# Splitting the first loads of a long-convolution block with a gated FFN, and writing its instruction order anew

## The chip, the cores and the metric

The kernel runs on one core of one Trainium2 chip. Its time is the device time of one execution in microseconds; where several executions were timed, the median is given.

## The reference

The input is a sequence of 2048 rows of 640 values (`q`, also the residual), with `k` and `v` of the same shape. With `LN` a layer norm without weights:

```python
q  = LN(x)                                   # x is A_q
ks = sum over t < 4 of shift(k, t) * shift_k[:, t]   # short causal convolution
kv = ks * v
y  = causal convolution of kv with ssm_k along the sequence + kv * ssm_D   # by FFT in the reference
h  = x + q * y
h2 = h + (silu(LN(h) @ w_gate) * (LN(h) @ w_up)) @ w_down   # 640 -> 1728 -> 640
```

Each of the 640 channels has its own filter `ssm_k` of 2048 taps. All tensors are bfloat16.

## The kernel before

The sequence is cut into four blocks of 512 rows, each laid over 128 partitions with four rows (r = 0 to 3) in each. The long convolution is done by blocks: each block of `kv` (X0 to X3) and of the filter (g0 to g3, transposed on TensorE by L431, the last by DMA) is taken to a spectrum of 512 real rows by matmuls with a table `WF` (L352), spectra are multiplied on VectorE (L591, L612, L615), summed over the pairs that meet in an output block, and taken back by matmuls with a table `WI` (L745). The short convolution is a set of small matmuls: `k`, transposed into a tile `T` (L533 and the copies L537 for block 0, DMA transposes for the others), times diagonal matrices `diag` that hold the taps (L978); the result times `v` is `kv`, made either by VectorE straight from PSUM (L578) or by a ScalarE copy (L579) and a VectorE product (L580). What TensorE leaves in PSUM goes to SBUF by ScalarE (L344, L435) or VectorE (L345, L435).

For block 0 the two spectra (X0, G0) and their products are worked in two halves of 320 channels, so that the first half can be multiplied while the second is transformed. The layer-norm sums are ScalarE's (L671, L628), their small arithmetic VectorE's (L643 to L653), the application either engine's (L682, L685).

Each finished block j goes through the FFN (f0 to f3): `LN(h)` is transposed (L783 on TensorE, L776 by DMA), multiplied by the gate and up weights (L846), passed through SiLU and product (L835, L837, L840), and multiplied by `w_down` (L915, L900). The FFN of block j - 1 is woven into the spectral work of block j; f3 comes last and alone.

Every instruction group is first entered into a list (`plan.add`, with an engine, an estimated length, and what it reads and writes). The table `ORDER` then gives the order in which the groups are issued; a negative number picks a group's other engine (VectorE in place of ScalarE, an accumulating DMA of GpSimd in place of a VectorE sum). Each engine runs its own instructions in that order. The large tiles share 13 slots (`big`), four PSUM tiles (`ps`) serve all matmuls, and a slot is handed out in the order of the table. So a new table changes the order on every engine, some engines, and the slots. The loads stand in the same table: `load` issues from SyncE's queue, and with an alternative from GpSimd's. SyncE issues in order, and an issue that waits for its slot holds up those behind it.

At the start TensorE turns over 34 idle matmuls (L959) until `k` has landed. Then come the transposes of `k`, those of g0, the short convolution, and the first forward transforms. In this kernel `k`, `g`, `v` and `WF` are loaded by one DMA each; `load_t` can cut a load by rows r, and `GPIECES` cuts the first g by groups of 128 channels, of which there are five.

Of the kernel before, what the change touches and what calls it, by code (L numbers as in the profile page):

```python
# [19 lines left out]
P = 128  # L20
# [18 lines left out]
GPIECES = ((0, KT),)  # L39
# [150 lines left out]
def kernel(ctx: ExitStack, tc: tile.TileContext, A_q, A_k, A_v, A_shift_k, A_ssm_k, A_ssm_D, B_x,  # L190
# [34 lines left out]
    def pe(ns, fn, r, w, holds=(), late=338):  # L225
        op = plan.add("pe", ns, fn, r, w, holds)
        op.late = late
        return op
# [278 lines left out]
    def load_k(j):  # L507

        if j == 0:
            return load_t(kk, 0)  # L510
# [471 lines left out]
    first("Lx0")  # L982
    x = load_x(0)
    first("Lv0")
    v = load_t(vv, 0)
    first("LWF")
    load(P * R * 4 * P * 2, 4096, lambda: nc.sync.dma_start(out=ap(WF), in_=wf_h.ap()), [WF])
    first("Lg0")
# [115 lines left out]
```

## Time and profile before

| | us |
|---|---|
| median of 3 runs | 257.15 (256.29 to 257.36) |
| profiled execution | 256.16 |
| its span, first to last instruction | 254.4 |
| mean granted TensorE clock | 0.993 |

The profile is one execution. A page gives the busy time of each engine: PE is TensorE's matmuls, PEld its weight loads (they overlap), DVE VectorE, ACT ScalarE, POOL GpSimd; SP is SyncE, which only issues DMAs. A row of the timeline gives the start, the length, the engine, the line of the kernel, the operation with its tiles (out<-in), and how often it was repeated; in square brackets the idle time ahead of it and what ended it. Rows of equal instructions that follow each other are merged.

### The profile page before, as it was taken

How to read it: one execution, taken by the hardware profiler on the slowest of the kernel's cores; microseconds unless marked ns; L12 is line 12 of the kernel's file. 1: busy time of each engine (PE TensorE's matmuls, PEld its weight loads, DVE VectorE, ACT ScalarE, POOL GpSimd, SP SyncE). 2: the span in 40 equal slices, each digit the busy share in tenths (PEclk: the TensorE clock that was granted, in tenths of full speed). 3: DMA queues.
4: the chain of work that ended last, by engine and by line, in shares of the span. 5: the costliest groups of instructions: out<-in, count | busy, mean ns of one | idle time of the engine just before them, and what ended most of it. 6: DMA issues, size and time to landing. Idle time of an engine off the chain costs nothing.

```text
span 254.4 us, 5139 instructions
## 1 busy us (share of the span) xinstructions
PE 246.7 (97%) x2070; PEld 145.2 (57%) x2070; DVE 192.1 (76%) x280; ACT 174.9 (69%) x306; POOL 67.4 (27%) x73
## 2 busy tenths in 40 slices
PE   8699999999999999999999999999999999999994
PEld 7566667744555576645554567544447744444663
DVE  0599999999989999999979999999998300102213
ACT  3969999998679899686788984348668144635200
POOL 6300020113444011149932013136920024000000
PEclk9799999999999999999999999999999999999999
DMA  6999777998897979898976386989973229000011
GB/s 239 350 356 234 196 203 141 211 249 199 159 330 199 176 169 183 205 200 207 278 142 119 83 126 119 187 192 212 211 158 80 58 46 131 0 0 0 3 41 62
DMA packets 51906, 41.04 MB, mean 161 GB/s; under 512 B 25461, under 2 KB 46202, under 8 KB 51882
## 3 DMA queue, kind: packets, MB, share of 16 engines
q1 hardware_dynamic: 45040, 26.94, 41.5%
q0 software_dynamic: 6832, 13.77, 30.5%
q8 instruction: 16, 0.26, 0.4%
q14 instruction: 8, 0.07, 0.1%
q10 hardware_dynamic: 10, 0.01, 0.0%
HBM read 22.03 MB, written 4.59 MB: 105 GB/s over the span
## 4 chain that ended last, share of the span: by engine, by line
PE 86%; ACT 6%; DMA 3%; DVE 2%; issue 1%; SPq 0%; DVEq 0%
PE ps L846 46%; PE ps L915 22%; PE ps L352 7%; ACT S L344 5%; PE ps L745 4%; PE ps L570 4%; DMA big<-in_A_ssm_k_dram 3%; PE ps L431 1%; PE ps L900 1%; DVE big L578 1%; ACT big L435 1%; ACT row L628 1%; DVE S L345 1%; ACT row L685 0%; ACT big L785 0%
## 5 line engine op out<-in xcount | busy, mean ns | idle before, releaser
L846 PE MATMUL ps<-big,big 128*128 128x512 bf16 x540 | 120.6, 379 | 0.0
L846 PEld LDWEIGHTS <-big 128*128 128x128 bf16 x540 | 52.0, 98 | 60.1 <-issue 0.5
L915 PE MATMUL ps<-wd,tT 128*128 128x320 bf16 (+2 forms) x416 | 59.5, 299 | 0.0
L915 PEld LDWEIGHTS <-tT 128*128 128x128 bf16 x416 | 40.3, 98 | 16.8 <-issue 1.3
L352 PE MATMUL ps<-big,WF 128*128 128x320 bf16 x224 | 37.0, 298 | 1.1 <-ACT S L344 0.4
L344 ACT ACTIVATE S<-ps 128x640 bf16<-128x640 f32 (+1 forms) x62 | 33.4, 620 | 4.3 <-PE ps L352 4.0
L612 DVE TENSOR_TENSOR big<-S,S 128x2560 bf16<-128x2560 bf16 x24 | 34.8, 1486 | 0.7 <-DMA S<-big 0.4
L835 ACT CAST co<-ps 128x1024 bf16<-128x1024 f32 x24 | 24.1, 1016 | 15.3 <-PE ps L846 15.1
L837 ACT ACTIVATE tT<-ps 128x1024 bf16<-128x1024 f32 x24 | 24.6, 1024 | 13.8 <-PE ps L846 13.7
L352 PEld LDWEIGHTS <-WF 128*128 128x128 bf16 x224 | 21.4, 97 | 12.7 <-issue 3.2
L628 ACT ACTIVATE row<-big 128x640 bf16<-128x640 bf16 x32 | 23.8, 752 | 2.2 <-DVE big L762 1.2
L840 DVE TENSOR_TENSOR tT<-tT,co 128x2048 bf16<-128x2048 bf16 x12 | 14.7, 1222 | 13.0 <-ACT co L835 9.0
L615 DVE TENSOR_TENSOR S<-S,big 128x2560 bf16<-128x2560 bf16 x16 | 23.4, 1486 | 0.1
L256 POOL DMA_DIRECT2D S<-big x9 | 10.9, 1210 | 46.0 <-DVE big L612 14.6
L685 ACT ACTIVATE row<-big,sm 128x640 bf16<-128x640 bf16 x22 | 19.6, 928 | 2.7 <-DVE sm L653 1.7
L858 DVE TENSOR_TENSOR tT<-tT,co 128x512 bf16<-128x512 bf16 x4 | 1.7, 422 | 21.7 <-ACT tT L856 21.3
L925 POOL DMA_DIRECT2D out_dram<-row x12 | 12.1, 1314 | 17.3 <-ACT row L924 17.2
L256 POOL DMA_DIRECT2D S<-S x4 | 5.7, 1431 | 38.2 <-ACT S L344 38.2
L924 ACT CAST row<-ps 128x640 bf16<-128x640 f32 x12 | 8.1, 690 | 10.3 <-PE ps L900 6.6
L759 DVE SCALAR_TENSOR_TENSOR row<-row,ps 128x640 bf16<-128x640 bf16 x16 | 12.8, 818 | 3.1 <-PE ps L745 2.9
L570 PEld LDWEIGHTS <-T 64*128 64x128 bf16 x640 | 12.0, 113 | 4.2 <-issue 4.0
L570 PE MATMUL ps<-diag,T 64*128 64x64 bf16 x640 | 13.5, 198 | 0.0
(93 smaller groups left out, 276.1 us busy)
## 6 DMA issues: line engine op xcount, KB each, us to landing
S<-big POOLq DMA_DIRECT2D x9, 640.0 KB, 6.3
big<-in_B_w_gate_dram SPq DMA_DIRECT2D x11, 320.0 KB, 5.6
big<-in_B_w_up_dram SPq DMA_DIRECT2D x10, 320.0 KB, 6.6
big<-in_A_q_dram SPq DMA_DIRECT2D x4, 640.0 KB, 5.5
big<-in_A_ssm_k_dram SPq DMA_DIRECT2D x4, 640.0 KB, 7.0
big<-in_A_v_dram SPq DMA_DIRECT2D x4, 640.0 KB, 4.3
S<-S POOLq DMA_DIRECT2D x4, 640.0 KB, 6.8
wd<-in_B_w_down_dram SPq DMA_DIRECT2D x1, 2080.0 KB, 12.2
```

The costliest lines, as they stand in the source:

```text
L256: nc.gpsimd.dma_start(out=to(), in_=what(), accum_op=ALU.add, max_dma_last_dim=2 * D * 2)
L344: plan.add("act", 700 if n else 430, lambda: nc.scalar.activation(dst(), src(), ACT.Copy, scale=by), [ps], [part], (), ("dve", 820 if n el ...
L352: nc.tensor.matmul(ap(ps)[:, h, 0:NH], ap(WF)[:, c, r, :], ap(src)[:, r, h * NH:(h + 1) * NH], start=(first and i == 0), stop=(last and i ...
L570: nc.tensor.matmul(out()[:, b, c, :], k, ap(diag)[at, c, t, :], start=(t == 0), stop=(t == 3))
L612: dve(1490, lambda b=b, xs=xs, hs=hs: nc.vector.tensor_mul(flat2(b), X.part(xs), H.part(hs)), [X.at(xs), H.at(hs)], [b], [A.b])
L615: f(A.part(dst), A.part(dst), flat2(b))
L628: act(825, lambda r=r, junk=junk: nc.scalar.activation(ap(junk), ap(x)[:, r, :], ACT.Square, scale=D ** -0.5, accum_out=sm(s, 1)[:, r:r + ...
L685: nc.scalar.activation(ap(row), ap(x)[:, r, :], ACT.Identity, bias=sm(s, 5)[:, r:r + 1], scale=sm(s, 4)[:, r:r + 1])
L835: act(1010, lambda ps=ps: nc.scalar.copy(ap(co)[:, at:at + 2, :], ap(ps)), src, [(co, gi % 2)])
L837: act(1010, lambda ps=ps: nc.scalar.activation(ap(tT)[:, c:c + 2, :], ap(ps), ACT.Silu), src, [done(range(c, c + 2), ROWS)])
L846: nc.tensor.matmul(ap(ps)[:, i, :], ap(w)[:, k, off:off + P], ap(hT)[:, k, :], start=(k == 0), stop=(k == KT - 1))
L915: nc.tensor.matmul(ap(ps)[:, hf, 0:n], ap(tT)[:, c, at:at + P], ap(wd)[:, c, col:col + n], start=j % 2 == 0 and c == order[0], stop=j % 2 ...
```

## The change

Four things change in the code. The first `k` and the first `v` are loaded in two pieces each (rows r = 0, 1 and rows 2, 3). The first `g` is loaded in two pieces, channel groups 0 and 1, and 2 to 4; its transposes wait for their own piece. `WF` is loaded in two pieces, table rows c = 0, 1 and c = 2, 3; a forward matmul waits for its half. The table `ORDER` is new throughout: it was searched for again with a model of the engines in which early pauses of TensorE count against an order. That search's model is not part of the kernel.

```diff
-GPIECES = ((0, KT),)
+GPIECES = ((0, 2), (2, KT))
...
 ORDER = [
-    0, 4, 2, 15, 1, 16, 5, 6, 19, 22, 20, 24, 26, 17, 18, 3, 23, 344, 9, 7, -26, -11, 28, -15, 353, 44, 29, 12, 200, 13,
...
+    16, 1, 15, 4, 23, 22, 0, 2, 5, 9, 6, 28, 7, 17, 32, 24, 30, 21, 3, 33, 19, 26, -30, -15, 55, 11, 20, 49, 31, 27, 48, 34,
...
-        pe(136 * len(ws) * len(rs), mm, [(src, r) for r in rs] + [WF] + ([] if first else [ps]), [ps], holds)
+        pe(136 * len(ws) * len(rs), mm, [(src, r) for r in rs] + [(WF, c // 2)] + ([] if first else [ps]), [ps], holds)
...
-            return load_t(kk, 0)
+            return load_t(kk, 0, 2)
...
-    v = load_t(vv, 0)
+    v = load_t(vv, 0, 2)
     first("LWF")
-    load(P * R * 4 * P * 2, 4096, lambda: nc.sync.dma_start(out=ap(WF), in_=wf_h.ap()), [WF])
+    for c in (0, 2):
+        load(P * R * 2 * P * 2, 2048, lambda c=c: nc.sync.dma_start(out=ap(WF)[:, c:c + 2], in_=wf_h.ap()[:, c:c + 2]), [(WF, c // 2)])
```

The lines of the new kernel stand one or two lower than those of the old (L352 becomes L353, L846 becomes L847, L987 becomes L989).

The table of numbers tells a reader little; the order on the engines tells more. First SyncE's queue at the start of the program, before. `big_72` takes k, `big_73` x (A_q), `big_74` g, `big_75` v.

```order
L317 DMA big_72<-in_A_k_dram 128x2560
L323 DMA big_73<-in_A_q_dram 128x2560
L309 DMA big_74<-in_A_ssm_k_dram 128x5x512
L317 DMA big_75<-in_A_v_dram 128x2560
L987 DMA WF<-const_wf 128x2048
L807 DMA big_76<-in_B_w_up_dram 128x5x256
L807 DMA big_77<-in_B_w_up_dram 128x5x256
L309 DMA big_79<-in_A_ssm_k_dram 128x5x512
```

The same place of SyncE's queue now; `big_73` takes g and `big_74` x.

```order
L318 DMA big_72<-in_A_k_dram 128x1280 x2
L310 DMA big_73<-in_A_ssm_k_dram 128x3x512
L310 DMA big_73<-in_A_ssm_k_dram 128x2x512
L324 DMA big_74<-in_A_q_dram 128x2560
L989 DMA WF<-const_wf 128x1024
L318 DMA big_75<-in_A_v_dram 128x1280
L989 DMA WF<-const_wf 128x1024
L318 DMA big_75<-in_A_v_dram 128x1280
L310 DMA big_78<-in_A_ssm_k_dram 128x5x512
```

g stands ahead of x, the halves of WF and v alternate, and the two early weight loads (`w_up`) have gone further back.

Second, VectorE from its first copy of `T` to the first normalisation steps, before. `big_78` is the transposed g, `big_80` kv, `S_64` and `S_65` the spectra of g and kv.

```order
L537 COPY T<-ps_93 128x5x128
L978 TENSOR_SCALAR diag<-row_88,taps 128x64 x8
L537 COPY T<-ps_95 128x5x128
L549 MEMSET T 128x20
L435 COPY big_78<-ps_94 128x640
L435 COPY big_78<-ps_96 128x640
L435 COPY big_78<-ps_94 128x640
L437 TENSOR_TENSOR big_78<-big_78,row_87 1x640
L435 COPY big_78<-ps_95 128x640
L578 TENSOR_TENSOR big_80<-ps_96,big_75 128x2x5x64
L578 TENSOR_TENSOR big_80<-ps_94,big_75 128x2x5x64
L345 TENSOR_SCALAR S_64<-ps_93 128x320
```

VectorE at the same place now; `big_76` is the transposed g, `big_77` kv.

```order
L538 COPY T<-ps_96 128x5x128
L979 TENSOR_SCALAR diag<-row_87,taps 128x64 x12
L436 COPY big_76<-ps_96 128x640
L550 MEMSET T 128x20
L436 COPY big_76<-ps_93 128x640
L436 COPY big_76<-ps_94 128x640
L438 TENSOR_TENSOR big_76<-big_76,row_88 1x640
L436 COPY big_76<-ps_95 128x640
L346 TENSOR_SCALAR S_64<-ps_94 128x320
L579 TENSOR_TENSOR big_77<-ps_96,big_75 128x2x5x64
L346 TENSOR_SCALAR S_64<-ps_94 128x320
L579 TENSOR_TENSOR big_77<-ps_93,big_75 128x2x5x64
```

One copy of T has gone to ScalarE, four products for `diag` have come from GpSimd, and a first eviction of g's spectrum stands ahead of the first product with v. Up to the end of block 0's inverse VectorE has eight evictions of this kind where it had six, and four products straight from PSUM where it had three.

Third, SyncE's queue where block 2's loads begin, now. `big_76` is a slot of FFN weights of block 0 that takes the next v, `big_73` and `big_84` are slots of later FFN weights, `big_79` takes x of block 2.

```order
L518 DMA_TRANSPOSE T<-in_A_k_dram 128x5x128 x3
L324 DMA big_79<-in_A_q_dram 128x2560
L318 DMA big_76<-in_A_v_dram 128x2560
L808 DMA big_84<-in_B_w_gate_dram 128x5x64
L808 DMA big_73<-in_B_w_gate_dram 128x5x256
L1028 DMA wd<-in_B_w_down_dram 64x640
```

Before, at that place:

```order
L517 DMA_TRANSPOSE T<-in_A_k_dram 128x5x128
L820 DMA out_dram<-big_73 128x2560
L807 DMA big_83<-in_B_w_up_dram 128x5x256
L309 DMA big_76<-in_A_ssm_k_dram 128x5x512
L807 DMA big_77<-in_B_w_gate_dram 128x5x256
L1023 DMA wd<-in_B_w_down_dram 128x13x640
```

The load of v for block 2 now stands ahead of two weight loads for the FFN of block 0. Between the last matmul on the old contents of `big_76` and the first on `big_73` TensorE has 30 FFN matmuls (L847) and 80 convolution matmuls. Late in the program, ahead of the first inverse matmul of block 3 (L745, now L746), TensorE has 130 of the 135 gate and up matmuls of f2, where it had 125, and VectorE one more product L840 (now L841) and one more sum L762 (now L763).

79 rows, old and new, of the table ORDER are left out of this document.

## The prediction

> **What bounds the kernel now.** I read the page's busy shares first, then the busy time of each engine in stretches cut where the shares change. The columns of a stretch are its length, then busy us (and instructions) of each engine, the granted TensorE clock, and the DMA share.
>
> ```profile
> PE 246.7 (97%) x2070; PEld 145.2 (57%) x2070; DVE 192.1 (76%) x280; ACT 174.9 (69%) x306; POOL 67.4 (27%) x73
> ...
> 5.00:9.40 4.40, 2.37 (x35) 1.94 (x35) 2.20 (x12) 3.11 (x8) 3.90 (x10) 0.96 0.97 333
> 9.40:12.60 3.20, 3.20 (x77) 2.92 (x75) 1.28 (x3) 3.20 (x10) 0.00 (x0) 0.52 1.08 362
> 12.60:30.00 17.40, 16.37 (x216) 11.11 (x209) 16.97 (x36) 15.26 (x40) 0.00 (x0) 1.00 1.11 288
> 30.00:50.00 20.00, 19.54 (x296) 14.37 (x294) 19.49 (x42) 19.63 (x36) 2.49 (x2) 1.00 0.83 169
> 50.00:190.00 140.00, 140.00 (x1063) 76.37 (x1061) 135.69 (x154) 107.97 (x178) 52.59 (x46) 1.00 0.88 188
> ```
>
> TensorE is busy 97% of the span, and from 50 us on without a gap, so nothing can be gained there; a new order can only lose. What can be gained lies in three places ahead of 50 us. Up to 9.4 TensorE stands idle for 2.0 of 4.4 us. From 9.4 to 12.6 it is busy but at 0.52 of its clock. From 12.6 to 50 VectorE (16.97 of 17.40, 19.49 of 20.00) and ScalarE are as full as TensorE: there the PSUM evictions and the spectral products pace it, and its "busy" holds waits inside the pipeline. The timeline of the front shows why.
>
> ```profile
> 0.79 0.40 SPq L317 DMA_DIRECT2D big<-in_A_k_dram  x1
> 1.25 0.41 SPq L323 DMA_DIRECT2D big<-in_A_q_dram  x1
> 1.72 0.43 SPq L309 DMA_DIRECT2D big<-in_A_ssm_k_dram  x1
> 2.18 0.75 SPq L317 DMA_DIRECT2D big<-in_A_v_dram  x1
> 2.98 0.45 SPq L987 DMA_DIRECT2D WF<-const_wf  x1
> 3.78 5.12 POOL L978 TENSOR_SCALAR diag<-row,taps 128x64 bf16<-128x64 bf16 x12 [1.26 <-DVE taps L970]
> 4.99 1.33 PE L533 MATMUL ps<-ident,big 128*128 128x128 bf16 x15
> 5.76 0.70 ACT L537 COPY T<-ps 128x640 bf16<-128x640 bf16 x1 [2.88 <-PE ps L533]
> 6.07 0.49 DVE L537 COPY T<-ps 128x640 bf16<-128x640 bf16 x1 [2.48 <-PE ps L533]
> 6.48 1.25 DVE L978 TENSOR_SCALAR diag<-row,taps 128x64 bf16<-128x64 bf16 x8
> 8.78 0.52 PE L431 MATMUL ps<-ident,big 128*128 128x128 bf16 x5 [1.83 <-DMA big<-in_A_ssm_k_dram]
> 9.23 1.25 PE L570 MATMUL ps<-diag,T 64*128 64x64 bf16 x40
> 10.41 1.79 PE L431 MATMUL ps<-ident,big 128*128 128x128 bf16 x15
> 12.65 0.47 DVE L437 TENSOR_TENSOR big<-big,row 1x640 bf16<-1x640 bf16 x1
> 13.45 1.53 DVE L578 TENSOR_TENSOR big<-ps,big 128x640 bf16<-128x640 f32 x2
> 13.57 1.16 PE L352 MATMUL ps<-big,WF 128*128 128x320 bf16 x6
> 16.48 0.76 PE L570 MATMUL ps<-diag,T 64*128 64x64 bf16 x40
> ```
>
> TensorE transposes k from 4.99, waits 1.83 us for g, and then meets the slow clock: 40 convolution matmuls take 1.25 us at 9.23 and 0.76 at 16.48. The first forward-transform matmul (L352) starts at 13.57, and VectorE's long unbroken run starts with the product at 13.45. When the loads land, the issues tell (last number: us from issue to landing).
>
> ```profile
> big<-in_A_k_dram SPq DMA_DIRECT2D x1, 640.0 KB, 3.9
> big<-in_A_q_dram SPq DMA_DIRECT2D x1, 640.0 KB, 5.1
> big<-in_A_ssm_k_dram SPq DMA_DIRECT2D x1, 640.0 KB, 7.0
> big<-in_A_v_dram SPq DMA_DIRECT2D x1, 640.0 KB, 8.1
> ...
> WF<-const_wf SPq DMA_DIRECT2D x1, 512.0 KB, 8.7
> ```
>
> Issue plus landing time: k at 4.7, q at 6.35, g at 8.7, v at 10.3, WF at 11.7. They come one after another: q 1.65 us after k, g 2.4 after q (its packets are shorter), v 1.6, WF 1.4.
>
> **The change part by part.** *The loads.* The new SyncE order is k in two pieces, g in two, q, then halves of WF and v in turn. With g straight behind k, its first piece (3 of 5 parts) lands about 4.7 + 1.45 = 6.1 and its second at 4.7 + 2.4 = 7.1, 1.6 us earlier; q then at 8.75, WF's first half at 9.45, v's first at 10.25, WF's second at 10.95, v's second at 11.75. The extra issues cost about 0.4 us each on SyncE's queue and all stand ahead of the data: with two more ahead of them g's last piece is issued at about 2.2. What a split costs in landing the trace does not show. From below it is nothing or a little gain (the 640 KB loads follow each other without a gap); from above I take one SyncE issue per piece, 0.45 us, and 0.9 for k and g together. I take nothing: g has that much cover, as the next step shows.
>
> *The front.* VectorE now does 12 of the diag products (1.25/8 = 0.156 each) and one copy of T; GpSimd does 8 instead of 12, and is done by 3.78 + 8 x 0.427 = 7.2. ScalarE does three T copies: 6.07 + 3 x 0.70 = 8.17. VectorE: T copy from 5.76 to 6.25, diag to 8.13, first g copy (0.49) to 8.62, a memset to 8.7, two more g copies to 9.68, the row addition 0.47 to 10.15, the last copy to 10.64. The g transposes are paced by PSUM buffers that these copies free, the last behind ScalarE's copy at 8.17, so g could land at 8.0 and cost nothing. The first convolution starts at 8.7, the second at 9.46, the first forward matmul at 10.2 against 13.57. VectorE's long run starts at 10.65 against 13.45: a lead of **2.8 us**. It needs v's first half at 11.1 (lands 10.25) and WF's second half near 11.8 (lands 10.95): covered, each by 0.8. GpSimd now issues a 320 KB weight load at about 7.3, right behind its diag products, which shares the DMA engines with these halves: half of q's 1.65 us, 0.8, if all of it went ahead, just the cover; the two w_up loads that stood behind WF on SyncE before come later instead.
>
> *The clock.* Before, the 1.83 us ahead of 8.78 are empty. Now the 20 g transposes fall there (5 took 0.52) and the convolution at 8.7 follows, so I expect no slow stretch. If it comes all the same, two convolutions take 1.25 instead of 0.76; VectorE's queue hides most of it, so the cost lies between 0 and 0.5 us. I take 0.
> The rule of the Trainium skill (TensorE: Matmul & The Clock Gate, "HAM oscillation — how this bites in real kernels") is that TensorE must not pause for more than about 3.4 us. The row differs: a pause of 1.83 us was followed by 3.2 us at 0.52, and the measurement decides; by the rule the pause would be worth its own 1.83 and no more, and the sum, which runs over VectorE, would be the same.
>
> *VectorE's run up to the inverse transform of block 0.* The new order gives VectorE work that ScalarE had.
>
> ```profile
> L345 DVE TENSOR_SCALAR S<-ps 128x320 bf16<-128x320 f32 x6 | 2.9, 485 | 0.1
> L762 DVE TENSOR_TENSOR big<-big,row 128x640 bf16<-128x640 bf16 x10 | 4.6, 487 | 0.0
> L682 DVE TENSOR_SCALAR row<-big,sm 128x640 bf16<-128x640 bf16 x10 | 4.1, 440 | 0.0
> L840 DVE TENSOR_TENSOR tT<-tT,co 128x2048 bf16<-128x2048 bf16 x12 | 14.7, 1222 | 13.0 <-ACT co L835 9.0 <-ACT tT L837 3.9
> ...
> 33.66 1.56 DVE L700 TENSOR_TENSOR S<-S 128x1280 bf16<-128x1280 bf16 x2
> 51.72 8.79 PE L846 MATMUL ps<-big,big 128*128 128x512 bf16 x40
> ```
>
> Between the first product and the end of L700 (35.2) there are two more evictions (2 x 0.485), one more product straight from PSUM (0.77 for the 0.48 of the sum it replaces), and one more normalisation (0.44): 0.97 + 0.29 + 0.44 = 1.7 us. Back-to-back rows overlap a little, so 1.5 to 1.7. Lead left: 2.8 - 1.5 = 1.3. Behind it block 1 has one PSUM product fewer on VectorE (0.3), and 0.5 us of VectorE's idle time between 30 and 50 was waiting for TensorE, which now has two block-1 convolutions and one transposition behind it already, 0.76 + 0.76 + 0.3 us: about half of that idle goes. Lead at the start of the FFN matmuls (L846 at 51.72): 1.3 + 0.3 + 0.25, about **1.8 us**.
>
> *From there to the end.* TensorE is full, its instructions are the same in number, so the lead is kept wherever each row is fed in time. The place to check is block 3's inverse, on which the last FFN waits.
>
> ```profile
> 185.75 1.56 DVE L718 TENSOR_TENSOR S<-S 128x1280 bf16<-128x1280 bf16 x2
> 187.39 0.71 PE L745 MATMUL ps<-S,WI 128*128 128x320 bf16 x4
> ...
> 206.81 29.31 PE L846 MATMUL ps<-big,big 128*128 128x512 bf16 x135
> ```
>
> TensorE took L745 0.08 us after VectorE had made its input: the two are level there. In the new order VectorE has one more L762-type sum (0.49) and one more L840-type product (1.22) ahead of it, 1.7 us against a lead of 1.8, so its input comes at about 187.2 less what it saves of the 4.3 us that it idled between 50 and 190; I take 0.4, so 186.8. TensorE now has five more FFN matmuls ahead of that place (5 x 0.217 = 1.1) and comes at 187.39 - 1.8 + 1.1 = 186.7. Loss 0.1. Sum: **1.7 us**. The profiled execution took 256.16 us, its span 254.4; the span becomes 252.7 and the execution 254.46. The median before, 257.15, is 0.99 above that execution, so the median after is about **255.4 us**, 0.7% less.
>
> **The rivals.** *VectorE does not catch up (R1).* If none of its idle time goes, block 3's input comes at 187.2 or later, TensorE waits there 0.5 us and more, and later stages of the new order may wait in the same way. For it: VectorE is busy 135.69 of 140. Against: the matmuls it waits for come earlier. Gain 0 to 1.2, middle 0.8: 256.3.
>
> *A weight load stuck behind another (R2, slower).* The new SyncE order has block 2's v load into big_76 ahead of the gate weights for big_73. It waits until the FFN has read big_76 for the last time, and from then to the first use of big_73 TensorE has 30 FFN matmuls and 80 convolution matmuls, 30 x 0.217 (29.31/135) + 2 x 0.76 = 8.0 us. Three issues at about 0.45 leave 6.6 us for landing. Over the run the L807 loads took:
>
> ```profile
> DMA to landing us min/median/max: 2.5/5.7/9.7
> ```
>
> At the median nothing happens; from 6.6 on TensorE stops, at 8 us by 1.4, at 9.7 by 3.1, and a stop of this length brought the slow clock before, which cost 3.2 x 0.48 = 1.5. So 257.15 - 1.7 + 1.4 + 1.5 = 258.4, at most 260.1. For it: v's 640 KB go ahead on the same queue. Against: the median.
>
> *The pieces come no sooner (R3).* If g's last piece lands at 8.7 as before, the g copies end about 1.3 us later than I have them; 1.7 - 1.3 and one slow stretch (0.5) leave nothing: 257.2. Against it: loads followed each other without a gap.
> The Trainium skill speaks for it (DMA: Bandwidth & Descriptors, "Rules for kernel authors"): it says to merge many small transfers into one; the page's fit for transfers of GpSimd ("Anatomy of one DMA — SWDGE (gpsimd) path") has about 2.0 us fixed in each. Were that paid in turn here, the four extra transfers would cost 8 us, an estimate from that page; no row here shows such a gap between queued loads.
>
> **How the numbers follow.** Forecast 0.60, R1 0.22, R2 0.12, R3 0.06. A median of three runs of this kernel tells about 0.5% (1.3 us, so 255.86 and 258.44) from no change. The forecast's own range is 254.4 to 256.2; 0.52 of its 0.60 lie below 255.86 and 0.08 above, R1 gives 0.03, 0.17 and 0.02, R2 0.02 and 0.10, R3 0.06 to the same. Faster 0.55, same 0.33, slower 0.12. For the range: low 253.4, where the whole front lead of 2.8 is kept and the 0.99 between median and profiled run goes too, if the slow clock is what makes some runs longer; high 258.2, over R1, R3 and the near half of R2.
>
> **What would show it.** Right: no wait of TensorE for g; clock near 1.00 from 9 to 13 us; the first forward matmul near 10.2; VectorE's L701 pair ends near 33.9; first FFN matmul plus the forward matmuls moved behind it level with about 49.9; no TensorE gap after 50. Wrong: a forward matmul later than 12, a row of TensorE waiting for VectorE near 187, or for a weight load between 55 and 75.

## The result and the profile after

The changed kernel takes **255.49 us** in the median of 21 executions (253.92 to 259.6), the kernel before 257.07 us in 21 (255.94 to 258.42). The ratio is 0.9937, with a 95% interval of 0.9915 to 0.9959. Ratios, here and below, leave out the executions that took over 1.5% more than the fastest of their kernel (four of these 21), while medians and ranges hold all. The profiled execution of the changed kernel took 254.12 us with a span of 252.4, against 256.16 and 254.4 before: 2.0 us less, where 1.7 had been forecast. Its mean granted clock is 1.000 (0.993 before). In the table below "end of block 0" is the end of the VectorE pair L701 (L700 before), "block 3" the first inverse matmul of block 3, "last FFN" the first gate and up matmul of f3.

| profiled execution | first forward matmul | end of block 0 | block 3 | last FFN |
|---|---|---|---|---|
| before | 13.57 | 35.22 | 187.39 | 206.81 |
| after | 10.42 | 33.73 | 186.38 | 204.71 |

The stretches of the changed kernel, with the columns as in the prediction (length, busy us and instructions of each engine, granted TensorE clock, DMA share, GB/s):

```profile
5.00:9.40 4.40, 3.03 (x66) 2.61 (x66) 3.17 (x17) 2.00 (x4) 2.33 (x7) 1.00 0.92 300
9.40:12.60 3.20, 2.55 (x78) 1.61 (x72) 2.86 (x7) 2.88 (x8) 0.00 (x0) 1.00 1.05 390
12.60:30.00 17.40, 17.07 (x196) 11.53 (x196) 17.05 (x34) 17.27 (x46) 0.96 (x1) 1.00 1.06 251
30.00:50.00 20.00, 19.27 (x286) 13.94 (x287) 19.59 (x43) 19.85 (x37) 2.48 (x2) 1.00 1.09 240
50.00:190.00 140.00, 139.21 (x1057) 77.18 (x1069) 135.58 (x155) 108.19 (x179) 51.03 (x48) 1.00 0.84 180
```

The slow stretch from 9.4 to 12.6 is gone (1.00 for 0.52), and VectorE is busy for 2.86 us of it where it was busy for 1.28. From 12.6 on the engines are as full as before. (Some matmul records are missing, 523 of 540 of L847 are there; the 139.21 is no sign of a gap, since the waits show none over 0.2 us there.) The timeline of the front and the end of block 0:

```profile
3.28 1.84 PE L960 MATMUL ps<-const-bfloat16-1.0 128*128 128x128 bf16 x16
...
4.96 1.28 PE L534 MATMUL ps<-ident,big 128*128 128x128 bf16 x20
...
6.84 0.53 PE L432 MATMUL ps<-ident,big 128*128 128x128 bf16 x6 [0.60 <-DMA big<-in_A_ssm_k_dram]
...
8.13 0.97 PE L432 MATMUL ps<-ident,big 128*128 128x128 bf16 x14 [0.77 <-DMA big<-in_A_ssm_k_dram]
...
9.04 1.34 PE L571 MATMUL ps<-diag,T 64*128 64x64 bf16 x80
...
10.42 0.45 PE L353 MATMUL ps<-big,WF 128*128 128x320 bf16 x2
...
10.90 0.49 DVE L346 TENSOR_SCALAR S<-ps 128x320 bf16<-128x320 f32 x1 [0.34 <-PE ps L353]
...
11.31 0.81 DVE L579 TENSOR_TENSOR big<-ps,big 128x640 bf16<-128x640 f32 x1
...
32.18 1.55 DVE L701 TENSOR_TENSOR S<-S 128x1280 bf16<-128x1280 bf16 x2
```

After the idle matmuls (L960) and the transposes of k (L534), TensorE still waits for g, twice (0.60 and 0.77 us), once for each piece. All 20 transposes of g are through by 9.1, both first convolutions run at full speed (80 matmuls in 1.34 us), and the first forward matmul comes 3.15 us earlier than before. Late in the program, VectorE and then TensorE at block 3's inverse and at the start of f3:

```profile
182.92 0.83 DVE L719 TENSOR_TENSOR S<-S 128x1280 bf16<-128x1280 bf16 x1
183.66 1.22 DVE L841 TENSOR_TENSOR tT<-tT,co 128x2048 bf16<-128x2048 bf16 x1
184.80 0.82 DVE L719 TENSOR_TENSOR S<-S 128x1280 bf16<-128x1280 bf16 x1
187.19 0.82 DVE L760 SCALAR_TENSOR_TENSOR row<-row,ps 128x640 bf16<-128x640 bf16 x1 [1.58 <-ACT co L858]
...
186.38 0.71 PE L746 MATMUL ps<-S,WI 128*128 128x320 bf16 x4
...
204.71 29.31 PE L847 MATMUL ps<-big,big 128*128 128x512 bf16 x132
```

VectorE has made the input of block 3's inverse by 185.62, 0.76 us before TensorE comes for it at 186.38, and then has time to spare. Before, the two were level (0.08 us).

### The profile page after: what moved, and what is told of

The parts are those of the page before. It is cut to its first block, busy times and chain, and to the rows that moved or that the text cites. A ratio compares the mean times of both kernels' runs of the same rounds, so it can differ in the third digit from the quotient of the medians.

```text
span 252.4 us, 5124 instructions
## 1 busy us (share of the span) xinstructions
PE 244.1 (97%) x2053; PEld 143.9 (57%) x2070; DVE 194.0 (77%) x288; ACT 172.8 (68%) x303; POOL 64.8 (26%) x73
## 4 chain that ended last, share of the span: by engine, by line
PE 87%; ACT 7%; DMA 2%; DVE 1%; issue 1%; SPq 0%
PE ps L847 46%; PE ps L916 23%; PE ps L353 7%; ACT S L345 6%; PE ps L571 5%; PE ps L746 4%; DMA big<-in_A_ssm_k_dram 2%; PE ps L901 1%; ACT big L436 1%; PE ps L432 1%; SPq L318 0%; DVE big L579 0%; ACT big L786 0%; DVE S L346 0%; DVE big L436 0%
## 5 line engine op out<-in xcount | busy, mean ns | idle before, releaser
L847 PE MATMUL ps<-big,big 128*128 128x512 bf16 x523 | 119.6, 379 | 1.0 <-issue 0.2
L847 PEld LDWEIGHTS <-big 128*128 128x128 bf16 x540 | 52.2, 98 | 59.9 <-issue 0.5
L353 PE MATMUL ps<-big,WF 128*128 128x320 bf16 x224 | 37.5, 299 | 1.0 <-DVE S L346 0.6
L345 ACT ACTIVATE S<-ps 128x640 bf16<-128x640 f32 (+1 forms) x60 | 32.3, 621 | 4.2 <-PE ps L353 3.8
L353 PEld LDWEIGHTS <-WF 128*128 128x128 bf16 x224 | 21.4, 97 | 13.3 <-issue 3.0
L616 DVE TENSOR_TENSOR S<-S,big 128x2560 bf16<-128x2560 bf16 x17 | 25.0, 1485 | 0.8 <-DMA S<-big 0.8
L841 DVE TENSOR_TENSOR tT<-tT,co 128x2048 bf16<-128x2048 bf16 x12 | 14.6, 1220 | 11.1 <-ACT co L836 11.0
L686 ACT ACTIVATE row<-big,sm 128x640 bf16<-128x640 bf16 x20 | 18.2, 944 | 0.2
L926 POOL DMA_DIRECT2D out_dram<-row x12 | 13.1, 1330 | 16.6 <-ACT row L925 16.6
L808 POOL DMA_DIRECT2D big<-in_B_w_gate_dram x6 | 7.9, 1322 | 26.6 <-DVE sm L654 18.1
```

The costliest lines, as they stand in the source:

```text
L345: plan.add("act", 700 if n else 430, lambda: nc.scalar.activation(dst(), src(), ACT.Copy, scale=by), [ps], [part], (), ("dve", 820 if n el ...
L353: nc.tensor.matmul(ap(ps)[:, h, 0:NH], ap(WF)[:, c, r, :], ap(src)[:, r, h * NH:(h + 1) * NH], start=(first and i == 0), stop=(last and i ...
L616: f(A.part(dst), A.part(dst), flat2(b))
L686: nc.scalar.activation(ap(row), ap(x)[:, r, :], ACT.Identity, bias=sm(s, 5)[:, r:r + 1], scale=sm(s, 4)[:, r:r + 1])
L841: dve(1220, lambda: nc.vector.tensor_mul(ap(tT)[:, c0:c0 + 4, :], ap(tT)[:, c0:c0 + 4, :], ap(co)), [co], [done(range(c0, c0 + 4), ROWS)])
L847: nc.tensor.matmul(ap(ps)[:, i, :], ap(w)[:, k, off:off + P], ap(hT)[:, k, :], start=(k == 0), stop=(k == KT - 1))
```

## The experiments

Ten altered kernels were run, one of them twice, and the changed kernel once more, each beside the kernel before on its chip; medians of the kernel before were 257.08, 256.66 and 256.9 us in the three groups, one per chip. The theory: the change gains its time in the front (g ahead of x, no long wait, no slow clock), and what follows keeps the lead. The rivals: the splits alone, the load order alone, the clock alone, or the later part of the new order.

### One part alone, on the kernel before

**g ahead of x.** The loads of g and x change places on SyncE; nothing else moves.

```diff
-for op in plan.schedule(ORDER):
+ops = plan.schedule(ORDER)
+ops.remove(plan.ops[19])
+ops.insert(ops.index(plan.ops[16]) + 0, plan.ops[19])
+for op in ops:
```

> The kernel before with one thing changed: the whole load of the first g is issued ahead of x (A_q); slots, splits and the order on every other engine stay. Theory (the gain of the change is made in the front, out of an earlier g and out of the slow clock that its wait brings): g lands near 7.3 to 8.1 instead of 8.74, TensorE's wait for it falls from 1.83 to 0.4 to 1.2 us, the clock from 9 to 13 us comes nearer to 1, the first forward matmul comes at 11.0 to 12.9 instead of 13.57, and the time falls by 0.6 to 1.5 us, to 255.6 to 256.5. Rival (the new order on VectorE and TensorE makes the gain, the loads alone nothing): the front moves by less than 0.5 us and the time stays at 257.1. Rival (x is needed early by ScalarE): ScalarE's first sums L671 come later and the time rises above 257.1.

Measured: 257.54 us, ratio 1.0021 (0.9993 to 1.0049): no gain, though the first forward matmul comes at 12.16 (13.57 before), as the theory had it. Rows of the timeline of this kernel, TensorE and ScalarE:

```profile
7.19 0.47 PE L431 MATMUL ps<-ident,big 128*128 128x128 bf16 x5 [0.42 <-DMA big<-in_A_ssm_k_dram]
...
9.07 0.74 ACT L671 ACTIVATE row<-big 128x640 bf16<-128x640 bf16 x1 [1.57 <-DMA big<-in_A_q_dram]
...
13.52 0.67 ACT L579 CAST big<-ps 128x640 bf16<-128x640 f32 x1
14.24 3.18 PE L352 MATMUL ps<-big,WF 128*128 128x320 bf16 x14 [1.63 <-ACT big L579]
```

The whole g lands at 7.2, about as early as the prediction had hoped for the second of its two pieces (7.1). But in the old order ScalarE does the sums over x (L671, L628) ahead of its copy of kv (L579), and x now lands later: ScalarE waits 1.57 us, the copy comes at 13.52, and TensorE stands for 1.63 us at 14.24. In the kernel before it came at 12.02:

```profile
12.02 0.67 ACT L579 CAST big<-ps 128x640 bf16<-128x640 f32 x1
```

The third expectation, that x is needed early by ScalarE, was right as to the wait; the rise of the time that it forecast is not clear of the interval. Here the load that came earlier for one engine made another come later, and the order on that other engine had not followed.

**The wait for g filled.** 15 idle matmuls ahead of the first transposes of g, in an unused part of their PSUM tile.

```diff
+FILL = 15
+FILLROW = 0
...
+if blk == 0 and r == FILLROW:
+    ones = nc.const_aps.tensor(1.0, [P, P], BF16)
+    for _ in range(FILL):
+        nc.tensor.matmul(ap(pt)[:, 1, 256:256 + P], ones, ones, start=True, stop=True)
```

> The kernel before, with 15 idle matmuls (as at the start) put on TensorE ahead of the first transposes of g, so that it is busy while it waits for g. They write an unused part of the PSUM tile; the loads and the order stay. g lands at 8.74 as before. Theory (the slow clock from 9.4 to 12.6 us is brought on by the 1.83 us pause and costs about 1.5 us of TensorE's front): the granted clock is 1.00 from 9.4 to 12.6, the first forward matmul comes at about 12.1 instead of 13.57, VectorE's long run starts 0.9 to 1.5 earlier, and the time falls by 0.9 to 1.5 us, to 255.6 to 256.2. Rival (the clock follows something else, such as the load of the memory or the time since the start): the clock in that stretch stays near 0.5 and the time stays at 257.1. Rival (VectorE's queue hides the slow stretch): clock 1.00, but the time within 0.5 us of 257.1.

Measured: 258.56 us, ratio 1.0063 (1.004 to 1.0085): slower, with no slow clock. The stretch, two rows of TensorE and one of VectorE's waits (us in all, times, the longest; the lines stand six lower here; L751 is the inverse, L618 a product of block 3):

```profile
9.40:12.60 3.20, 3.11 (x129) 2.90 (x131) 2.04 (x5) 3.20 (x9) 0.00 (x0) 1.00 1.06 364
```

```profile
9.38 0.47 PE L437 MATMUL ps<-ident,big 128*128 128x128 bf16 x5 [2.04 <-DMA big<-in_A_ssm_k_dram]
...
189.71 0.72 PE L751 MATMUL ps<-S,WI 128*128 128x320 bf16 x4 [1.30 <-DVE S L724]
```

```profile
DVE big L618 <- DMA S<-big: 2.7, 1, 2.7
```

The clock stays at 1.00 and the first forward matmul comes at 12.88 (13.57 before), but block 0 ends at 35.38, no earlier than before (35.22). g landed 0.6 us later in this execution (9.38 for 8.78), which took a part of what the clock gave; and behind the first forward matmuls TensorE waits for VectorE's products, 0.30 us at 14.34 and 0.69 at 15.73. Then block 3's product waits 2.7 us for a sum that a DMA of GpSimd accumulates, and TensorE 1.30 us for VectorE at block 3's inverse, where the old order has no slack. So a front without the slow clock gained nothing in front of the old order. The executions of the kernel before say much the same: in the three groups, those with a mean clock of 0.998 or more have a median of 256.5 us (23, without one of 887 us), those near 0.993 (as in the profiled execution, with its one slow stretch) one of 256.7 (58). Only the 12 at 0.987 are clearly longer: 257.7.

**The splits alone.** The code of the changed kernel with the old order, pieces next to each other.

```diff
-ORDER = [the new order]
+ORDER = [the old order, the pieces of each load and of each transposition of g next to each other]
```

> The splits alone: the code of the changed kernel with the whole order of the kernel before, the pieces of each load next to each other (k, k, x, g, g, v, v, WF, WF). Theory (splits alone do nothing, since g is waited for all the same and each piece needs its own issue): g's last piece lands 0 to 0.9 us later than 8.74, and the time is 257.0 to 258.0. Rival (the splits carry the gain): 255.5 to 256.2.

Measured: 257.14 us, ratio 1.002 (0.9991 to 1.0049). The splits alone gain nothing, and those of k and g, both ahead of g's last piece here, cost landing time:

```profile
8.97 0.40 PE L432 MATMUL ps<-ident,big 128*128 128x128 bf16 x2 [2.42 <-DMA big<-in_A_ssm_k_dram]
10.16 0.51 PE L432 MATMUL ps<-ident,big 128*128 128x128 bf16 x3 [0.80 <-DMA big<-in_A_ssm_k_dram]
```

The second piece of g is there at 10.16, 1.4 us after the whole g of the kernel before (8.74).

### Front and rest exchanged

The new order issues 298 groups ahead of the first FFN matmul. Two hybrids take the order of these from one kernel and the order of all others from the other.

```diff
-ORDER = [the new order]
+ORDER = [298 groups in the new order] + [the others in the old order]
```

> A hybrid order on the code of the changed kernel (loads split): the 298 groups that the new order issues ahead of the first FFN matmul stand in the new order; all groups behind them stand in the order of the kernel before. Theory (the change gains its 1.6 us in the front, and what follows only has to keep it): 255.3 to 256.0, with the first FFN matmul as early as in the changed kernel. Rival (the later part of the new order makes or keeps the gain; in the kernel with the idle matmuls, block 3's inverse waited 1.3 us for VectorE in the old order): front as early as in the changed kernel, a TensorE wait near 187, and 256.5 to 257.5.

Measured: 257.66 us, ratio 1.0003 (0.9968 to 1.0037), from 254.94 to 259.9. In the profiled execution (span 256.6) block 0 ends at 33.72, as early as in the changed kernel, and the lead is then lost in two waits of TensorE:

```profile
78.38 1.25 PE L746 MATMUL ps<-S,WI 128*128 128x320 bf16 x8 [1.52 <-DVE row L760]
...
162.79 17.43 PE L847 MATMUL ps<-big,big 128*128 128x512 bf16 x80 [1.85 <-DMA big<-row]
```

The second of them is for `LN(h)` of block 2, transposed by DMA. The rival was right in its mechanism, not in its place: no wait stands near 187, and the waits that took the lead in this execution lie elsewhere. In the median, a front that is 1.5 us ahead gains nothing in front of the old order.

```diff
-ORDER = [the new order]
+ORDER = [the same 298 groups in the old order] + [the others in the new order]
```

> The opposite hybrid: the same 298 groups in the order of the kernel before (with the loads split, pieces next to each other, in the old order k, x, g, v, WF), and all groups behind them in the new order. Theory (the gain is made in the front): 256.6 to 257.4, as before, with a first forward matmul at 13 to 13.6. Rival (the later part makes the gain, by the slack that VectorE has at block 3's inverse): 255.3 to 256.0.

Measured: 257.76 us, ratio 1.0033 (1.0004 to 1.0061). Its front is that of the splits alone (first forward matmul at 15.64, end of block 0 at 36.80), later than the kernel before and than expected, so the fair comparison is with the splits alone (1.002): against them too the later part gains nothing. So neither half carries the gain; it is there when both are.

### Parts of the changed kernel undone

**All four loads whole.** `GPIECES`, `load_k`, `v` and `WF` as before, in the new order.

```diff
-GPIECES = ((0, 2), (2, KT))
+GPIECES = ((0, KT),)
...
-v = load_t(vv, 0, 2)
+v = load_t(vv, 0)
```

> The changed kernel with its four loads whole again (k, g, v and WF by one DMA each, in the order k, g, x, WF, v, where the first pieces stood); the rest of its order stays. Theory (the halves of WF and v come just in time, the pieces of g matter little): WF lands about 0.6 us later and v about 0.8 us later than their first halves did, VectorE's first product comes 0.5 to 1.3 us later, and the time is 0.4 to 1.3 us above the changed kernel's 255.5: 255.9 to 256.8. Rival (the splits carry the whole gain): 257.1 or more. Rival (the splits cost: g's two pieces took 3.5 us behind k, where the whole g took 2.4 behind x in the kernel before): g lands near 7.3 instead of 8.1, and the time is the same or less, 254.7 to 255.5.

Measured: 256.37 us, ratio 0.9963 (0.9932 to 0.9995). A gain is there without any split; whether it is all of the 0.63% or a small part, the interval leaves open. TensorE in this kernel:

```profile
4.74 2.34 PE L534 MATMUL ps<-ident,big 128*128 128x128 bf16 x20
7.14 1.31 PE L432 MATMUL ps<-ident,big 128*128 128x128 bf16 x20
...
12.57 0.43 PE L353 MATMUL ps<-big,WF 128*128 128x320 bf16 x2 [0.77 <-DVE big L579]
```

g is there without a wait at 7.14, where the pieces came by 6.84 and 8.13. (That no wait shows is also due to the transposes of k, which took 2.34 us in this execution, for 1.28 in the changed kernel.) The price is paid behind: the whole v lands later, and TensorE waits 0.77 us for its product. Against 0.9937 of the changed kernel the difference of 0.26% is within the intervals.

**k and g whole, v and WF in halves.**

```diff
-GPIECES = ((0, 2), (2, KT))
+GPIECES = ((0, KT),)
...
-return load_t(kk, 0, 2)
+return load_t(kk, 0)
```

> The changed kernel with k and g whole again, v and WF in halves as in the change. With all four whole, g had landed by 7.1 with no wait of TensorE for it, the first forward matmul came at 10.07, and then TensorE waited 0.8 us for a product with v. Theory (two pieces of g cost about 1 us of its landing, the halves of v and WF earn about 0.6): no wait for g, first forward matmul near 10.1, no wait for v, and 0.2 to 0.6 us less than the changed kernel: 254.9 to 255.3. Rival (VectorE and ScalarE set the pace there, g's landing has cover): 255.5, no different from the changed kernel.

> The changed kernel with k and g whole, v and WF in halves, once more beside the changed kernel: theory 0.2 to 0.6 us less than the changed kernel and fewer long executions; rival: no difference beyond 0.2 us.

> The changed kernel once more, for a comparison on one chip: 255.0 to 255.8, with some executions above 257.

Measured: first 254.84 us, ratio 0.9918 (0.9889 to 0.9948, 6 executions); then, on one chip, 254.94 and 0.9939 (0.9906 to 0.9971) beside the changed kernel's 254.97 and 0.9938 (0.9915 to 0.9962). It does not beat the changed kernel. Its front is earlier still:

```profile
7.17 1.31 PE L432 MATMUL ps<-ident,big 128*128 128x128 bf16 x20 [1.07 <-DMA big<-in_A_ssm_k_dram]
8.41 1.34 PE L571 MATMUL ps<-diag,T 64*128 64x64 bf16 x80
9.69 0.44 PE L353 MATMUL ps<-big,WF 128*128 128x320 bf16 x2
```

The first forward matmul comes 0.73 us ahead of the changed kernel's and block 0 ends at 32.96 (33.73), but in this execution the last FFN begins at 204.48 (204.71): of 0.77 us, 0.23 are left. TensorE stands for 0.43 us at 105.58, for an eviction of ScalarE by the profile, where the changed kernel begins f1 without a wait at 105.82: most of the lead is lost there.

**Block 2's v behind the weight loads** (rival R2).

```diff
-for op in plan.schedule(ORDER):
+ops = plan.schedule(ORDER)
+ops.remove(plan.ops[437])
+ops.insert(ops.index(plan.ops[377]) + 1, plan.ops[437])
+for op in ops:
```

> The changed kernel with one thing changed: the load of v for block 2 is issued behind the two weight loads of block 0 that stood behind it on SyncE's queue. The changed kernel's executions lie between 253.9 and 259.6 us, wider than the 255.9 to 258.4 of the kernel before. Theory that the weight loads stuck behind v (the rival R2 of the prediction) make the long executions: now all lie within about 1 us of the shortest, and the median falls to 254.5 to 255.0. Theory that R2 never decides, as the profile with no wait of TensorE there shows: median and spread as of the changed kernel, 255.5, with some executions above 257.

Measured: 255.43 us, ratio 0.994 (0.9911 to 0.9969): no difference, and one execution of 259.75 us among the 12. The weight loads behind v do not make the long executions. What its profiled execution has is a wait that those of the changed kernel do not have (us in all, times, the longest), behind an operation of ScalarE:

```profile
PE ps L571 <- ACT tT L838: 1.6, 1, 1.6
```

**The front held up.** 40 instead of 16 idle matmuls ahead of the transposes of k.

```diff
-WARMUP = (18, 16)
+WARMUP = (18, 40)
```

> The changed kernel with 40 instead of 16 idle matmuls in the second group ahead of the transposes of k: TensorE's front is held up on purpose by about 24 x 0.115 = 2.8 us, of which the wait for g (0.8 + 0.8 us in the changed kernel) takes up a part. No long pause, so the clock stays at 1.00. Theory (a delay of the front passes to the end, since VectorE runs without a gap from there): first forward matmul near 11.7 instead of 10.42, and the time rises by the same 1.2 to 1.3 us, to 256.5 to 257.0. Rival (the new order has slack behind the front that takes it up): less than 0.4 us more, 255.4 to 255.8.

Measured: 257.05 us, ratio 0.9992 (0.996 to 1.0025), against 254.97 for the changed kernel on the same chip.

```profile
6.81 1.28 PE L534 MATMUL ps<-ident,big 128*128 128x128 bf16 x20
...
11.26 0.45 PE L353 MATMUL ps<-big,WF 128*128 128x320 bf16 x2
```

```profile
33.21 1.55 DVE L701 TENSOR_TENSOR S<-S 128x1280 bf16<-128x1280 bf16 x2
```

The transposes of k start 1.85 us later, the wait for g takes up a part, and the first forward matmul comes 0.84 us later than in the changed kernel (0.60 later than in its execution on this chip, 10.66). That delay was half to two thirds of what was expected; block 0 ends at 34.76, 1.0 us later than in the changed kernel's first execution and 0.5 later than in the other. The time rose by about 1.4 us (0.9992 against 0.9938), more than the delay: in its profiled execution 0.82 us of waiting ahead of f1 come on top. So the new order did not take the delay up here; how much of the rise the delay alone makes, the next experiment leaves open.

**A pause ahead of k.** 1 instead of 16 idle matmuls.

```diff
-WARMUP = (18, 16)
+WARMUP = (18, 1)
```

> The changed kernel with 1 instead of 16 idle matmuls in the second group ahead of the transposes of k, so that TensorE pauses for about 1.5 us ahead of them; all else stays. Theory (a pause of 1.5 us and more brings about 3 us of half clock, as the 1.83 and 1.63 us pauses did in other kernels, and the 0.77 us ones of the changed kernel did not): the clock is near 0.5 for about 3 us between 5 and 9, the transposes of k and g take twice as long there; g's late landing covers part of it, so the first forward matmul comes 0.3 to 0.9 us later and the time is 255.7 to 256.3. Rival (the clock does not follow the pause): clock 1.00 and 255.4.

Measured: 255.18 us, ratio 0.9944 (0.9914 to 0.9974): as the changed kernel.

```profile
4.72 2.31 PE L534 MATMUL ps<-ident,big 128*128 128x128 bf16 x20 [1.37 <-DMA big<-in_A_k_dram]
6.83 0.85 PE L432 MATMUL ps<-ident,big 128*128 128x128 bf16 x6
8.14 1.43 PE L432 MATMUL ps<-ident,big 128*128 128x128 bf16 x14 [0.47 <-DMA big<-in_A_ssm_k_dram]
...
187.51 0.71 PE L746 MATMUL ps<-S,WI 128*128 128x320 bf16 x4
```

```profile
33.32 1.55 DVE L701 TENSOR_TENSOR S<-S 128x1280 bf16<-128x1280 bf16 x2
```

Time and granted clock are the rival's, but not its reason: the clock reads 1.00 throughout, yet the 20 transposes of k take 2.31 us for 1.28, and 14 of g 1.43 for 0.97. The wait for g hides most of it: the first forward matmul comes at 10.78. But block 0 ends at 34.87, as late as with 40 idle matmuls (34.76), after VectorE has waited 1.0 us for a convolution; block 3's inverse comes at 187.51, 1.13 us later than in the changed kernel's first execution, so in this trace the delay is carried through, with no wait ahead of f1. And yet the median is the changed kernel's. What a delay of about 1 us in front of the new order costs is therefore not settled: the two kernels with it stand at 0.9992 and 0.9944, with intervals that overlap a little.

### What one longer execution shows

The changed kernel spread from 253.9 to 259.6 us. The execution that was profiled when it ran again (256.54 us) had a span of 254.8, 2.4 us more than the first; longer ones were not traced. Of the 2.4 us, 0.5 are there at the end of block 0 (34.26 for 33.73), and the rest comes at one chain. GpSimd's accumulating DMAs and TensorE in the longer execution:

```profile
66.17 1.26 POOL L257 DMA_DIRECT2D S<-S  x1
79.03 1.20 POOL L257 DMA_DIRECT2D S<-S  x1 [11.61 <-DMA S<-S]
...
108.26 1.24 PE L847 MATMUL ps<-big,big 128*128 128x512 bf16 x4 [1.81 <-DMA big<-row]
```

The same in the first:

```profile
66.30 1.26 POOL L257 DMA_DIRECT2D S<-S  x1
77.62 1.20 POOL L257 DMA_DIRECT2D S<-S  x1 [10.05 <-DMA S<-S]
...
105.82 1.25 PE L847 MATMUL ps<-big,big 128*128 128x512 bf16 x4
```

The second sum is issued when the first has landed, which took 12.3 us instead of 10.8. VectorE then waits 0.7 us for the second sum, the layer norm of block 1 and its four DMA transposes start at 99.07 instead of 97.81, and TensorE waits 1.81 us for them ahead of f1. The chain of waits of this execution (start, us, what) runs through both sums; that of the shorter one does not:

```profile
66.17 12.33 DMA S<-S
79.03 6.97 DMA S<-S
```

The same wait ahead of f1 stands in the profiled executions of the kernel with 40 idle matmuls (0.82 us) and of the second run with k and g whole (1.49, with a further 1.3 us of waiting for VectorE in the last FFN). Why the sum takes longer in some executions, and what makes the longest ones, stays open.

## Why the prediction was right, point by point

Of its signs, the clock, the first forward matmul, the end of L701, the start of the FFN and, in the first profiled execution, the full TensorE behind 50 us came as forecast; "no wait of TensorE for g" did not (0.60 and 0.77 us).

- **The loads: the order was right, the landing of g was off by 1.0 us.** Forecast were 6.1 and 7.1 for the pieces, with the price of the split bounded at 0.9 and taken as nothing. They were there at about 6.8 and 8.1, while the whole g in the same place came by 7.2. The splits of k and g together cost 0.9 to 1.1 (TensorE took the last of g at 8.13 and 8.30 with both split, at 7.17 and 7.21 with both whole), the upper bound or a little more; which of the two splits costs it, no run shows. The cover that the prediction gave it ("g could land at 8.0 and cost nothing") was not where it was put: the copies of T that were to pace the transposes were done by 7.6, TensorE waited for g itself, and with g whole the first forward matmul came 0.73 us and the end of block 0 0.77 us earlier. That the time was no shorter comes from behind, where that lead went. R3 had the sign of the split right, not the size (the last piece came at 8.1, not at 8.7), and not the consequence. The rule of the Trainium skill that speaks for R3 (DMA: Bandwidth & Descriptors, "Rules for kernel authors") agrees in sign with these pieces of 256 to 384 KB; the loss was about 1 us for two extra transfers, and no run shows the 8 us for four that the estimate from the page's fixed cost gave.
- **No GpSimd load beside the halves.** The prediction had a weight load issued at about 7.3 from GpSimd. In the changed kernel's trace GpSimd stands there for 18 us and issues it at 25.46; nothing waited for it:

```profile
25.46 0.96 POOL L808 DMA_DIRECT2D big<-in_B_w_gate_dram  x1 [18.13 <-DVE sm L654]
```

- **The front.** First forward matmul 10.42 against 10.2, VectorE's run from 10.90 against 10.65: a lead of 2.55 instead of 2.8.
- **The clock.** No slow stretch, as forecast; why it stayed away is not shown, since pauses of 0.60 and 0.77 us were left and length alone does not decide (below). The idle matmuls showed that without a slow stretch the old order gains nothing, which fits "VectorE's queue hides most of it".
- **VectorE's extra work.** The run from its start to the end of L701 is 33.73 - 10.90 = 22.83 us, before 35.22 - 13.45 = 21.77: 1.06 more instead of 1.5. The lead there is 1.5 against 1.3 forecast. The first FFN matmul comes at 47.13 with 20 forward matmuls moved behind it, 20 x 0.143 (4.00/28, from the row of 28 before) = 2.9: level with 50.0, where 49.9 was forecast.
- **The catch-up at block 3 was mis-sized.** The prediction let VectorE save 0.4 us of its idle time between 50 and 190 and 0.25 ahead of that. From the end of block 0 to the end of the last L718 or L719, before and after:

```profile
35.20:187.31 152.11, 151.94 (x1303) 86.07 (x1298) 147.41 (x185) 119.70 (x201) 54.53 (x47) 1.00 0.90 189
```

```profile
33.73:185.62 151.89, 150.37 (x1218) 85.38 (x1230) 148.62 (x186) 120.06 (x202) 51.35 (x48) 1.00 0.88 189
```

  VectorE did 1.2 us more work in 0.2 us less: its idle time fell from 4.7 to 3.3 us, by 1.4. The input came at 185.62, not 186.8, and the loss of 0.1 became a slack of 0.76. R1 did not happen at that place.
- **Where the reasoning was too simple.** "TensorE is full, so the lead is kept" named block 3 as the one place to check. The hybrid with the new front and the old rest shows that fullness keeps nothing: waits of 1.5 to 1.9 us open at other places when a chain behind the lead does not come forward with it. In the changed kernel one such place is the start of f1: it has no wait in one profiled execution and 1.81 us in the other. R1 had the mechanism ("later stages of the new order may wait in the same way"), not the place.
- **R2** did not decide: no wait for a weight load in either trace of the changed kernel, and moving v behind them changed nothing.
- **The sum.** 2.55 - 1.06 = 1.5 at the end of block 0, 2.1 at the last FFN (206.81 - 204.71), 2.0 of the span, against 2.8 - 1.5 = 1.3 and 1.7. The median fell by 1.58, less than the span between the two profiled executions; the wait at f1, which comes and goes, may be the reason. That 255.4 was met to 0.1 is partly luck: a front 0.25 us worse than forecast met a VectorE run 0.44 better, the profiled execution was 0.34 below its forecast, and the distance from it to the median 1.37 instead of 0.99.

## What to carry to other kernels

Bringing a load forward is worth what the order behind it lets through: g ahead of x, the splits, the clock and each half of the order gained nothing by themselves here, the new order without the splits 0.4% (0.05 to 0.7), and all together 0.6%. When a lead is claimed for a full engine, list every chain that must come forward with it (accumulating DMAs and DMA transposes included), and the slack at each place where it rejoins. Of a split, ask first whether the piece that is waited for is the first or the last; for g it was the last, and with k and g cut in two it came 1 us later than whole.

## What the runs showed of the hardware

- **The length of a pause does not decide on the slow clock.** A pause of 1.83 us (before) and one of 1.63 us (g ahead of x) were followed by a stretch near half clock. One of 2.04 us after 15 idle matmuls was not (1.00 from 9.4 to 12.6), and neither was the 1.81 us ahead of f1 (1.00 from 108 to 114). The Trainium skill (TensorE: Matmul & The Clock Gate, "What's actually happening") has a free-running window of activity, by which the place of a pause in the window would matter; no run here shows the window.
- **The granted clock does not show the warm-up.** Idle matmuls at the start took 1.84/16 = 0.115 us each at a granted clock of 1.00; the transposes of k then took 1.28/20 = 0.064 us in the changed kernel, but 2.31/20 = 0.115 with one idle matmul instead of 16, and 2.34/20 = 0.117 in the kernel with all loads whole, which has the 16. So the number of idle matmuls is not all that decides; the clock reads 1.00 in all of them. The same page and section say that what is issued in the first 3.4 us or so runs at half speed. The durations show a slow start, but a longer one: TensorE starts at 0.83, and the durations fall to half at about 5.0 in the changed kernel and at 7.1 with all loads whole.
- **What goes with a slow stretch differs from order to order.** In the kernel with g ahead of x, executions with a mean clock near 0.993 took 257.45 to 259.21 us (7), those at 1.000 256.01 to 256.85 (4), with medians of 258.1 and 256.65. In the kernel before, the difference between the same two groups is 0.2 us.
